# Second MLP: down products of two token blocks as seven products of 256 columns, in all four groups

## Chip, core and metric

The kernel runs on one NeuronCore of a Trainium2 chip. The metric is the device time of one execution in microseconds (us); of several runs the median is given. TensorE (PE) multiplies matrices, VectorE (DVE) and ScalarE (ACT) do elementwise work, SyncE (SP) issues the DMAs, GpSimd (POOL) works only in the first stage here.

## The reference, cut

```
out = decayed linear attention of q, k, v with lam
x   = out as [1536 tokens, 512]
x   = g1(x @ moe_w_in) @ moe_w_out     # [512, 2048], g1(h) = h * tanh(softplus(h)), [2048, 512]
y   = g2(x @ moe2_w_in) @ moe2_w_out   # the same shapes, g2(h) = max(h, 0) ** 2
```

All in 32-bit floats. The two MLPs are layers L = 0 and L = 1 of the kernel.

## The kernel before, in words

**Numbers in two parts.** Each operand of a product is held as a high part (a copy rounded to the matmul's type, made by ScalarE) and a low part (the difference, made by VectorE); `split` (L292) issues the two. `mm3` (L282) makes of each product three matmuls: high by low, low by high, high by high. All matmuls of the MLPs are issued at L289, all plain copies of ScalarE at L277 and all sums and differences of two tensors by VectorE at L280, so the tiles' names tell them apart in the trace.

**Tiles.** The 1536 tokens are three blocks t = 0, 1, 2 of 512. The inner width of 2048 is four groups g of 512. A *unit* is an SBUF tile of 128 x 1024 words of 4 bytes, and there are 51 (`UNITS`, L34). A PSUM tile is also 128 x 1024, over two banks, and there are four. For each layer and group: `weights` (L517) loads two units of each weight (kind 0 is w_in, kind 1 is w_out; the loads have 64-bit elements, which ScalarE, tile m, and VectorE, tile t, bring into 32 bits at L551, L556 and L563) and splits them into wh, wl. `up` (L677) makes the up products of block 0. `up_pair` (L725) makes those of blocks 1 and 2 together by seven products in place of eight, in the manner of Strassen: sums and differences of quarters of the weight (`sums`, L575, tiles s, sh, sl) meet sums and differences of quarters of the tokens (`forms`, L618, tiles T, fh, fl), and the products are put together in PSUM, on top of copies made by ScalarE (`seed`, L750) or by VectorE's sums. `gated` (L655) applies the activation.

**Down products.** `down` (L793) makes for one block two results (d = 0, 1), each of 24 matmuls for each of two units u. From the second group on, ScalarE first copies the sum so far from SBUF into PSUM (`onto`, L800), the matmuls add to it, and ScalarE copies it back (ac). For groups in `PAIRS` (L37: layer 0, groups 1 to 3) blocks 1 and 2 go instead through `down_pair` (L854): seven products again, each with a split of its own (eh, el), with the kind-1 sums of `sums` and the differences D of the gated units, and six sums kept from group to group (`keep`, tiles ap and ac). In layer 1 no group is in `PAIRS`: there blocks 1 and 2 go through `down`, 48 matmuls of 512 columns for each block and group, with tokens on the partitions of the result.

**Forms.** The 14 units fh, fl of a layer stay in SBUF in its first groups. From group `SPILL[L]` on (L39: 2 for layer 0, 9, which is never, for layer 1) `load_form` (L611) fetches each from DRAM just before its product, at most 14 us ahead (`BACK`); `store_form` (L605) has put them there (L608).

**Order.** No order is written by hand for most engines. Every operation is given to `Plan` (L64) with an engine, an estimated time, what it reads and writes, and for PE a rank; `ranks` (L962) counts them up. `dues` (L108) derives for every other operation the latest start that keeps PE going in rank order. `run` (L130) then plays the engines forward: PE takes the ready operation of lowest rank, another engine the one that is due first among those due within 40 us (`AHEAD`) for which a unit is free. A weight load of SP starts only if 10 units beside its own stay free, and the two operations that unpack it only if 6 do (`SPARE`, L41, L546, L559). The order so found is each engine's fixed queue.

**Sequence.** Per group: up of block 0, up_pair, then down of block 0 and either down_pair or down of blocks 1 and 2. Group (0, 0) goes block by block. `TURNED` (L29) is empty: a group in it would take up_pair ahead of up, and down_pair ahead of down. In the last group of layer 1 the last block handled is the tail (L795): its results come in halves of 512 columns, VectorE adds each to the sum so far, and SP stores it.

Of the kernel before, what the change touches and what calls it, by code (L numbers as in the profile page):

```python
# [25 lines left out]
TB = 512  # L26
WARM = 8
GF = 4
TURNED = ()  # L29

RANGE = 2.0 ** -112
BELOW = 2.0 ** 32
# [1 line left out]
UNITS = 51  # L34
STRASSEN = (True, True)
PLAIN = ((0, 0),)
PAIRS = ((0, 1), (0, 2), (0, 3))  # L37
DEBUG = None
SPILL = (2, 9)  # L39
BACK = 14.0  # L40
SPARE = (10, 6)  # L41
AHEAD = 40.0
# [21 lines left out]
class Plan:  # L64
# [7 lines left out]

    LAG = {"PE": 0.35, "DVE": 0.2, "ACT": 0.3, "POOL": 0.25, "SP": 3.8}

    def __init__(self, ahead):
        self.ops, self.ahead = [], ahead
        self.wrote, self.used, self.orders = {}, defaultdict(list), set()

    def op(self, eng, us, fn, reads=(), writes=(), name="", rank=None, lag=None, due=None, spare=0, ahead=None):
        o = Op(eng, us, fn, name, rank, self.LAG[eng] if lag is None else lag, due, spare)  # L80
        o.ahead = ahead or self.ahead.get(eng)
        for x in reads:
            o.before[self.wrote[x]] = None
        for x in writes:
            o.before.update(dict.fromkeys(self.used[x]))
            if x in self.wrote:
                o.before[self.wrote[x]] = None
        for x in reads:
            self.used[x].append(o)
        for x in writes:  # L90
            self.wrote[x], self.used[x] = o, []
        for x in (*reads, *writes):
            if isinstance(x[0], Val):
                o.vals[x[0]] = None
        for v in o.vals:
            v.left += 1
        for b in o.before:
            b.after[o] = None
        self.ops.append(o)
        return o  # L100
# [29 lines left out]
    def run(self, start, units):  # L130
# [5 lines left out]
        for o in self.ops:  # L136
            if not left[o]:
                o.at = 0.0
                ready[o.eng].append(o)
        releases, order, last = [], [], {}  # L140

        turn = {}
        for o in sorted((o for o in self.ops if o.eng == "PE"), key=lambda o: o.rank):
# [13 lines left out]
        while n < len(self.ops):  # L157
            while releases and releases[0][0] <= now:
                _, v = releases.pop(0)
                free[v.space].append(v.slot)  # L160
            for e in ready:
                if clock[e] > now:
                    continue
                can = [o for o in ready[e] if o.at <= now and (e == "PE" or o.late - now < o.ahead)]
                if not can:
                    continue
                best = None
                for o in sorted(can, key=lambda o: o.rank if e == "PE" else o.late):
                    need = defaultdict(int)
                    for v in o.vals:  # L170
                        if v.slot is None:
                            need[v.space] += 1
                    if any(v.seeded and v.slot is None and not fits(v) for v in o.vals):
                        continue
                    if o.eng != "PE" and need["P"] and next(v for v in turn if v.slot is None) not in o.vals:
                        continue
                    if all(len(free[s]) >= k + (o.spare if s == "S" else 0) for s, k in need.items()):
                        best = o
                        break
                if best is None:  # L180
                    continue
                o = best

                if e != "PE" and any(q.at > now and q.at < now + 0.7 * o.us and q.late < o.late - 2.0
                                     for q in ready[e]):
                    continue
                for v in sorted((v for v in o.vals if v.slot is None), key=lambda v: v.name):
                    v.slot = fits(v)[0]
                    free[v.space].remove(v.slot)
                    if v.space == "P":  # L190
                        last[v.slot] = v
                o.start, o.end = now, now + o.us
                clock[e] = o.end
                ready[e].remove(o)
                order.append(o)
                n += 1
                for v in o.vals:
                    v.left -= 1
                    v.was = max(v.was or 0.0, o.end + o.lag)
                    if not v.left:  # L200
                        bisect.insort(releases, (v.was, v), key=lambda r: r[0])
                for a in o.after:
                    left[a] -= 1
                    if not left[a]:
                        a.at = max(b.end + (b.lag if (b.eng != a.eng or b.lag > 1) and (b, a) not in self.orders else 0.0)
                                   for b in a.before)
                        ready[a.eng].append(a)
            times = [c for c in clock.values() if c > now]
            times += [o.at for r in ready.values() for o in r if o.at > now]
            times += [r[0] for r in releases[:1]]  # L210
            times += [o.late - o.ahead + 1e-6 for e in ready if e != "PE" for o in ready[e]
                      if o.late - o.ahead + 1e-6 > now]
            times = [t for t in times if t > now]
            if not times:
                stuck = [o.name for r in ready.values() for o in r][:20]
                held = sorted({v.name for o in self.ops for v in o.vals if v.slot is not None and v.left and v.space == "S"})
                raise RuntimeError(f"stuck {held} at {now} with {n} of {len(self.ops)}: {stuck} {len(free['S'])} {len(free['P'])}")
            now = min(times)
# [5 lines left out]
def attention_mlps(ctx, tc, lam, qk, kv, w_in, w_out, w2_in, w2_out, out):  # L224
# [292 lines left out]
    def weights(L, g, kind, kk):  # L517
# [4 lines left out]
        for i in range(2):  # L522
# [33 lines left out]
                    nc.vector.tensor_scalar(out=tl(t)[o, i], in0=tl(st, TB, 2)[r, :, 0], scalar1=29, scalar2=None,  # L556
                                            op0=ALU.logical_shift_right)

            op("ACT", 0.67 * len(rows()), high, [(st, 0)], [(m, i)], name=f"m{name}{i}", spare=SPARE[1])  # L559
            op("DVE", 0.45 * len(rows()), low, [(st, 0)], [(t, i)], name=f"t{name}{i}", spare=SPARE[1])  # L560

        def join():
# [92 lines left out]
    def gated(L, g, t, u, h, in_psum):  # L655

        name = f"{L}{g}{t}{u}"
        if not in_psum:
            op("ACT", 1.05, lambda: nc.scalar.activation(out=tl(h), in_=tl(h), func=AF.Relu if L else AF.Mish),
               [(h, 0)], [(h, 0)], name=f"r{name}")  # L660
        if L:
            op("ACT", 1.05, lambda: nc.scalar.activation(out=tl(h), in_=tl(h), func=AF.Square),
               [(h, 0)], [(h, 0)], name=f"sq{name}")
        if t and (L, g) in PAIRS:
            h_raw[L, g, t, u] = h
            return
        hi, lo = Val(f"gh{name}", dtype=F32R), Val(f"gl{name}", dtype=F32R)
        g_hi[L, g, t, u], g_lo[L, g, t, u] = hi, lo
        split(hi, lo, h, [(h, 0)])

    def take(L, g, t, u, src):
        h = Val(f"h{L}{g}{t}{u}")
        op("ACT", 1.05, lambda: nc.scalar.activation(out=tl(h), in_=tl(src), func=AF.Relu if L else AF.Mish),  # L673
           halves(src), [(h, 0)], name=h.name)
        gated(L, g, t, u, h, True)

    def up(L, g, t, rank):  # L677
# [114 lines left out]

    def down(L, g, t, rank):  # L793
        final = g == NG - 1
        tail = final and L == 1 and t == NB - 1  # L795
        for d in range(2):

            outs = [product_unit(f"dn{L}{g}{t}{d}{i}", not tail) for i in range(2 if tail else 1)]
            o = outs[0]
            onto = g > 0 and not tail  # L800
            if onto:
                a = accs[L, t, d]
                o.seeded = True
# [50 lines left out]
    def down_pair(L, g, rank):  # L854
# [1 line left out]
        b11, b21, b12, b22 = (h_raw[L, g, t, u] for t in (1, 2) for u in (0, 1))  # L856
        final = g == NG - 1
        opening = accs.get((L, "p"), None) is None
        if opening:
            c11, c21, c12, c22 = (accs[L, t, d] for t in (1, 2) for d in range(2))  # L860
            op("DVE", 1.25, lambda: tt(tl(c12), tl(c12), tl(c22), ALU.subtract), [*halves(c12), *halves(c22)],
               halves(c12), name=f"-c12{L}{g}")
# [8 lines left out]
        def product(i, raw, o):  # L871
# [7 lines left out]
            for s in range(2):  # L879
                def products(s=s):  # L880
                    for k in range(2):
                        f = slice(s * P, (s + 1) * P)
                        mm3(tl(o)[:, s], view(lh)[:, k, f], view(ll)[:, k, f], tl(rh)[:, k], tl(rl)[:, k],
                            k == 0, k == 1, onto=onto)

                reads = [(x, 0) for x in (lh, ll, rh, rl)] + ([(o, s)] if onto else [])
                op("PE", 1.37, products, reads, [(o, s)], name=f"Q{i}{L}{g}{s}", rank=rank + n[0])
                n[0] += 1
            return o

# [18 lines left out]
        def keep(i, o):  # L909
            a = acc[i] = acc[i] if i in acc else Val(f"ap{L}{i}")  # L910
            op("ACT", 1.05, lambda: copy(tl(a), tl(o)), halves(o), halves(a), name=f"k{i}{L}{g}")
            return a

        def result(t, d, o):
            a = x_raw[1, t, d] = Val(f"xr1{t}{d}")
            op("ACT", 1.05, lambda: copy(tl(a), tl(o)), halves(o), halves(a), name=a.name)

        sub(t3, b22, b12)
        sub(t1, b12, b11)
        sub(t2, b22, t1)  # L920
        sub(t4, b21, t2)
        a = product(1, b11, None)
        b = plus(a, acc[2], "b")
        if not final:
            keep(3, product(3, b22, seed(3)))
            product(2, b21, b)
# [20 lines left out]
        plus(a, acc[4])  # L947
        product(4, t4, a)
        result(1, 1, a)
        c = x_raw[1, 2, 1] = Val("xr121")  # L950
        op("DVE", 1.25, lambda: tt(tl(c), tl(e), tl(f), ALU.add), [*halves(e), *halves(f)], halves(c), name=c.name)
        plus(e, acc[3])
        product(3, b22, e)
        result(2, 0, e)
# [115 lines left out]
```

## Time and profile before

| | |
|---|---|
| median of 3 runs | 550.01 us (549.73 to 550.61) |
| the profiled execution's own time | 551.3 us |
| its span | 549.5 us |
| PE busy | 540.9 us (98%), 2950 matmuls |
| PE weight loads busy | 447.5 us (81%) |
| VectorE busy | 320.4 us (58%) |
| ScalarE busy | 373.3 us (68%) |
| DMA | 71.77 MB, mean 131 GB/s |

The span is the profiled part of an execution; its own time, 1.8 us longer, lies around it. In the tables by stage a figure in brackets behind a busy time is the number of instructions, PEclk is the granted clock of TensorE as a share of 2.4 GHz, and DMA is the mean busy share of the 16 DMA engines. A tile is named without its buffer's number, so dn<-wh,gl is a matmul that writes a down result from the moving tile wh and the stationary tile gl. The duration of a matmul contains its way through the array, and the matmuls overlap; the pace is the distance of two starts.

### The profile page before, as it was taken

The numbers are of one execution on the slowest core, as the hardware profiler recorded it, in microseconds if no ns is written. First come the engines' busy times: TensorE is split into PE (matmuls) and PEld (weight loads), VectorE is DVE, ScalarE is ACT, GpSimd is POOL, SyncE is SP. The second block draws the span as 40 slices with busy tenths as digits, with TensorE's granted clock in tenths as the row PEclk, the third lists the DMA queues.
The fourth block names the chain that finished last, engine by engine and source line by source line (L and its number), as shares of the span: only waits on it lengthen the run. The fifth ranks groups of instructions, "written<-read, shape, count | busy, mean of one in ns | idle before, by whom it ended". The sixth has DMA issues, their size and how long they took to land.

```text
span 549.5 us, 7237 instructions
## 1 busy us (share of the span) xinstructions
PE 540.9 (98%) x2950; PEld 447.5 (81%) x2950; DVE 320.4 (58%) x353; ACT 373.3 (68%) x413; POOL 31.8 (6%) x32
## 2 busy tenths in 40 slices
PE   7999999999999999999999999999999999999997
PEld 5898788888888888888878888888888888888885
DVE  6848686562686739787498886424361455333302
ACT  3637566593878789688995887458962898457920
POOL 2666100000000000000000000000000000000000
PEclk9999999999999999999999999999999999999999
DMA  8998003702799426971404021121134010300123
GB/s 313 408 409 251 3 0 114 269 1 76 285 335 410 140 57 199 348 246 48 154 0 154 1 78 38 51 103 39 38 116 151 3 38 1 115 2 1 38 78 115
DMA packets 20515, 71.77 MB, mean 131 GB/s; under 512 B 2306, under 2 KB 2306, under 8 KB 20482
## 3 DMA queue, kind: packets, MB, share of 16 engines
q1 hardware_dynamic: 20480, 71.31, 36.7%
q8 instruction: 23, 0.38, 0.3%
q14 instruction: 10, 0.08, 0.0%
q10 hardware_dynamic: 2, 0.00, 0.0%
HBM read 60.82 MB, written 10.49 MB: 130 GB/s over the span
## 4 chain that ended last, share of the span: by engine, by line
PE 91%; ACT 4%; DMA 2%; DVE 1%; issue 1%; SPq 0%; ACTq 0%
PE dn L289 34%; PE up L289 20%; PE p L289 13%; PE e L289 7%; PE b L289 4%; PE o L289 4%; PE q L289 3%; PE xo L455 2%; PE sc L413 2%; DMA qk<-in_qk_dram 2%; PE xo L464 1%; PE sd L436 1%; ACT L551 1%; ACT eh L277 1%; ACT h L673 1%
## 5 line engine op out<-in xcount | busy, mean ns | idle before, releaser
L280 DVE TENSOR_TENSOR gl<-h,gh 128x1024 fp32r<-128x1024 f32 x36 | 45.5, 1267 | 59.6 <-ACT gh L277 59.3
L277 ACT ACTIVATE ac<-dn 128x1024 f32<-128x1024 f32 x34 | 34.9, 1027 | 62.2 <-PE dn L289 60.9
L289 PE MATMUL dn<-wl,gh 128*128 128x512 f32 x192 | 74.7, 389 | 0.0
L289 PE MATMUL dn<-wh,gl 128*128 128x512 f32 x192 | 74.7, 389 | 0.0
L289 PE MATMUL dn<-wh,gh 128*128 128x512 f32 x192 | 74.7, 389 | 0.0
L563 DVE SCALAR_TENSOR_TENSOR t<-m,t 128x1024 int32<-128x1024 int32 x32 | 39.8, 1249 | 44.9 <-ACT m L551 44.7
L280 DVE TENSOR_TENSOR wl<-t,wh 128x1024 fp32r<-128x1024 f32 x32 | 38.8, 1222 | 21.3 <-ACT wh L277 21.2
L551 ACT ACTIVATE m<-st 128x512 f32<-128x512 f32 (+1 forms) x66 | 42.1, 665 | 6.7 <-DMA st<-in_moe_w_in_dram 6.5
L289 PEld LDWEIGHTS dn<-wl,gh 128*128 128x128 f32 x192 | 36.0, 188 | 7.5
L289 PEld LDWEIGHTS dn<-wh,gl 128*128 128x128 f32 x192 | 36.0, 188 | 7.5
L289 PEld LDWEIGHTS dn<-wh,gh 128*128 128x128 f32 x192 | 36.0, 188 | 7.4
L673 ACT ACTIVATE h<-up 128x1024 f32<-128x1024 f32 x20 | 20.5, 1027 | 26.6 <-PE up L289 26.6
L277 ACT ACTIVATE gh<-h 128x1024 fp32r<-128x1024 f32 x36 | 37.8, 1054 | 0.5
L289 PE MATMUL dn<-gl,wh 128*128 128x512 f32 x96 | 37.3, 389 | 0.0
L289 PE MATMUL dn<-gh,wl 128*128 128x512 f32 x96 | 37.3, 389 | 0.0
L289 PE MATMUL dn<-gh,wh 128*128 128x512 f32 x96 | 37.3, 389 | 0.0
L277 ACT ACTIVATE wh<-t 128x1024 fp32r<-128x1024 f32 x32 | 33.4, 1050 | 5.0 <-DVE t L563 4.9
L280 DVE TENSOR_TENSOR sl<-s,sh 128x1024 fp32r<-128x1024 f32 x20 | 24.2, 1222 | 8.1 <-ACT sh L277 8.0
L289 PE MATMUL up<-xh,wh 128*128 128x512 f32 (+1 forms) x80 | 28.0, 350 | 0.0
L289 PE MATMUL up<-xl,wh 128*128 128x512 f32 (+1 forms) x80 | 27.8, 348 | 0.0
L289 PE MATMUL up<-xh,wl 128*128 128x512 f32 (+1 forms) x80 | 27.7, 346 | 0.0
L556 DVE TENSOR_SCALAR t<-st 128x512 int32<-128x512 int32 (+1 forms) x66 | 26.6, 438 | 0.1
(167 smaller groups left out, 1244.6 us busy)
## 6 DMA issues: line engine op xcount, KB each, us to landing
st<-in_moe_w_out_dram SPq DMA_DIRECT2D x32, 512.0 KB, 4.1
st<-in_moe_w_in_dram SPq DMA_DIRECT2D x26, 512.0 KB, 5.3
fh<-f SPq DMA_DIRECT2D x14, 512.0 KB, 7.1
fl<-f SPq DMA_DIRECT2D x14, 512.0 KB, 7.1
qk<-in_qk_dram SPq DMA_DIRECT2D x12, 512.0 KB, 10.3
kv<-in_kv_dram SPq DMA_DIRECT2D x12, 512.0 KB, 10.4
f<-fh SPq DMA_DIRECT2D x7, 512.0 KB, 6.3
f<-fl SPq DMA_DIRECT2D x7, 512.0 KB, 6.2
```

The costliest lines, as they stand in the source:

```text
L277: nc.scalar.activation(out=o, in_=i, func=AF.Copy)
L280: nc.vector.tensor_tensor(out=o, in0=a, in1=b, op=alu)
L289: nc.tensor.matmul(out=out_, lhsT=a, rhs=b, start=start, stop=pieces or (last and i == 2), skip_group_check=not start if pieces else onto)
L413: nc.tensor.matmul(out=o[:, e, p], lhsT=t[r, 1, p], rhs=t[r, 0, p], start=True, stop=True)
L436: nc.tensor.matmul(out=o[e * D : (e + 1) * D, p], lhsT=t[:, p, 1 + e], rhs=t[:, p, 0 if e else 3], start=True, stop=True)
L455: nc.tensor.matmul(out=o[weighted(p, e), p, n], lhsT=v[:, p, 0 if e else 3], rhs=w[:, e, p], start=p % 2 == n == 0, stop=True, skip_group_ ...
L464: nc.tensor.matmul(out=o[weighted(h, e), h, n], lhsT=z[r, h], rhs=qd[r, h], start=False, stop=True, skip_group_check=True)
L551: nc.scalar.activation(out=tl(m)[o, i], in_=tl(st, TB, 2)[r, :, 1].bitcast(F32), func=AF.Prelu, scale=RANGE, alpha=BELOW)
L556: nc.vector.tensor_scalar(out=tl(t)[o, i], in0=tl(st, TB, 2)[r, :, 0], scalar1=29, scalar2=None, op0=ALU.logical_shift_right)
L563: nc.vector.scalar_tensor_tensor(out=tl(t), in0=tl(m).bitcast(I32), scalar=3, in1=tl(t), op0=ALU.logical_shift_left, op1=ALU.bitwise_or)
L673: op("ACT", 1.05, lambda: nc.scalar.activation(out=tl(h), in_=tl(src), func=AF.Relu if L else AF.Mish), halves(src), [(h, 0)], name=h.name)
```

## The change

Layer 1 joins `PAIRS` in all four groups: blocks 1 and 2 go through `down_pair`. There each of its seven products has, for layer 1, gated tokens as the stationary operand (blocks of 128) and 256 columns of weights as the moving one, 24 matmuls of 256 columns for a product where layer 0 has 12 of 512. Group (1, 0) has no earlier sums: its second accumulator starts as ScalarE's copy. The results of the last group go to the output straight from `down_pair` (four stores of 512 KB, rows of 1 KB). Block 0 of layer 1 is no longer accumulated in PSUM: VectorE adds each result to the sum (`ADDED`). Where a gated unit of layer 1 does not come from PSUM, one VectorE operation makes both relu and square. Layer 1's forms are stored and fetched again from its group 2 on (`SPILL`). Group (1, 3) is turned. The planner counts 1.5 us for a change of ScalarE's function table and ranks an operation that needs one 4 us later.

```diff
@@ -26,7 +26,8 @@
 GF = 4
-TURNED = ()
+TURNED = ((1, 3),)
+ADDED = (False, True)
@@ -34,9 +35,9 @@
 PLAIN = ((0, 0),)
-PAIRS = ((0, 1), (0, 2), (0, 3))
+PAIRS = ((0, 1), (0, 2), (0, 3), (1, 0), (1, 1), (1, 2), (1, 3))
 DEBUG = None
-SPILL = (2, 9)
+SPILL = (2, 2)
 BACK = 14.0
@@ -72,13 +73,15 @@
+    SWITCH = (1.5, 4.0)
+
     def __init__(self, ahead):
...
-    def op(self, eng, us, fn, reads=(), writes=(), name="", rank=None, lag=None, due=None, spare=0, ahead=None):
+    def op(self, eng, us, fn, reads=(), writes=(), name="", rank=None, lag=None, due=None, spare=0, ahead=None, table=None):
         o = Op(eng, us, fn, name, rank, self.LAG[eng] if lag is None else lag, due, spare)
-        o.ahead = ahead or self.ahead.get(eng)
+        o.ahead, o.table = ahead or self.ahead.get(eng), table
         for x in reads:
@@ -137,7 +140,7 @@
                 ready[o.eng].append(o)
-        releases, order, last = [], [], {}
+        releases, order, last, table = [], [], {}, None
@@ -165,7 +168,8 @@
                 best = None
-                for o in sorted(can, key=lambda o: o.rank if e == "PE" else o.late):
+                for o in sorted(can, key=lambda o: o.rank if e == "PE" else o.late + (
+                        self.SWITCH[1] if o.table and o.table != table else 0.0)):
                     need = defaultdict(int)
@@ -190,6 +194,8 @@
                 o.start, o.end = now, now + o.us
+                if o.table and o.table != table:
+                    o.end, table = o.end + self.SWITCH[0], o.table
                 clock[e] = o.end
@@ -556,7 +562,7 @@
-            op("ACT", 0.67 * len(rows()), high, [(st, 0)], [(m, i)], name=f"m{name}{i}", spare=SPARE[1])
+            op("ACT", 0.67 * len(rows()), high, [(st, 0)], [(m, i)], name=f"m{name}{i}", spare=SPARE[1], table="prelu")
             op("DVE", 0.45 * len(rows()), low, [(st, 0)], [(t, i)], name=f"t{name}{i}", spare=SPARE[1])
@@ -655,10 +661,13 @@
         name = f"{L}{g}{t}{u}"
-        if not in_psum:
+        if L and not in_psum:
+            op("DVE", 1.25, lambda: nc.vector.scalar_tensor_tensor(
+                out=tl(h), in0=tl(h), scalar=0.0, in1=tl(h), op0=ALU.max, op1=ALU.mult), [(h, 0)], [(h, 0)], name=f"rs{name}")
+        elif not in_psum:
             op("ACT", 1.05, lambda: nc.scalar.activation(out=tl(h), in_=tl(h), func=AF.Relu if L else AF.Mish),
-               [(h, 0)], [(h, 0)], name=f"r{name}")
-        if L:
+               [(h, 0)], [(h, 0)], name=f"r{name}", table=None if L else "mish")
+        if L and in_psum:
             op("ACT", 1.05, lambda: nc.scalar.activation(out=tl(h), in_=tl(h), func=AF.Square),
@@ -671,7 +680,7 @@
         op("ACT", 1.05, lambda: nc.scalar.activation(out=tl(h), in_=tl(src), func=AF.Relu if L else AF.Mish),
-           halves(src), [(h, 0)], name=h.name)
+           halves(src), [(h, 0)], name=h.name, table=None if L else "mish")
         gated(L, g, t, u, h, True)
@@ -792,12 +801,12 @@
         final = g == NG - 1
-        tail = final and L == 1 and t == NB - 1
+        tail = final and L == 1 and t == (0 if (L, g) in PAIRS else NB - 1)
         for d in range(2):
...
             o = outs[0]
-            onto = g > 0 and not tail
+            onto = g > 0 and not tail and not ADDED[L]
             if onto:
@@ -856,7 +865,9 @@
         opening = accs.get((L, "p"), None) is None
-        if opening:
+        if opening and not g:
+            accs[L, "p"] = {}
+        elif opening:
             c11, c21, c12, c22 = (accs[L, t, d] for t in (1, 2) for d in range(2))
@@ -879,12 +890,18 @@
                     for k in range(2):
+                        if L:
+                            for j in (2 * s, 2 * s + 1):
+                                f = slice(j * P, (j + 1) * P)
+                                mm3(tl(o, 4, 2 * P)[:, j], tl(rh)[:, k, f], tl(rl)[:, k, f], view(lh)[:, k], view(ll)[:, k],
+                                    k == 0 and j == 2 * s, k == 1, onto=onto, pieces=True)
+                            continue
                         f = slice(s * P, (s + 1) * P)
...
                 reads = [(x, 0) for x in (lh, ll, rh, rl)] + ([(o, s)] if onto else [])
-                op("PE", 1.37, products, reads, [(o, s)], name=f"Q{i}{L}{g}{s}", rank=rank + n[0])
+                op("PE", 1.42 if L else 1.37, products, reads, [(o, s)], name=f"Q{i}{L}{g}{s}", rank=rank + n[0])
                 n[0] += 1
@@ -911,16 +928,26 @@
+        def done(t, d, a):
+            if not L:
+                x_raw[1, t, d] = a
+                return
+            r = slice(t * TB, (t + 1) * TB)
+            op("SP", 1.3, lambda: nc.sync.dma_start(
+                out=out[r, d * 2 * P : (d + 1) * 2 * P].rearrange("(b p) c -> p b c", p=P), in_=tl(a, 4, 2 * P)),
+               halves(a), [("out", t, d)], name="out")
+
         def result(t, d, o):
-            a = x_raw[1, t, d] = Val(f"xr1{t}{d}")
+            a = Val(f"xr{L}{t}{d}")
             op("ACT", 1.05, lambda: copy(tl(a), tl(o)), halves(o), halves(a), name=a.name)
+            done(t, d, a)
...
         a = product(1, b11, None)
-        b = plus(a, acc[2], "b")
+        b = plus(a, acc[2], "b") if 2 in acc else copied(a, "b")
         if not final:
@@ -947,8 +974,9 @@
         result(1, 1, a)
-        c = x_raw[1, 2, 1] = Val("xr121")
+        c = Val(f"xr{L}21")
         op("DVE", 1.25, lambda: tt(tl(c), tl(e), tl(f), ALU.add), [*halves(e), *halves(f)], halves(c), name=c.name)
+        done(2, 1, c)
         plus(e, acc[3])
```

## Rows read from the trace of the kernel before

**Rows 1.** The page's busy times: engine, us, share of the span, instructions.

```profile
PE 540.9 (98%) x2950; PEld 447.5 (81%) x2950; DVE 320.4 (58%) x353; ACT 373.3 (68%) x413; POOL 31.8 (6%) x32
```

**Rows 2.** Busy times by stage of PE's order, us from the span's start.

```profile
core 0: us, PE busy (x) PEld busy (x) DVE busy (x) ACT busy (x) POOL busy (x), PEclk, DMA share, GB/s
13.67:71.76 58.09, 56.43 (x785) 48.62 (x786) 42.39 (x50) 34.88 (x52) 28.57 (x23) 1.00 0.69 254
...
175.12:234.96 59.84, 59.84 (x265) 49.55 (x265) 42.70 (x47) 49.67 (x53) 0.00 (x0) 1.00 0.60 204
234.96:281.95 46.99, 46.57 (x205) 38.19 (x205) 35.24 (x36) 42.25 (x44) 0.00 (x0) 1.00 0.36 118
281.95:325.47 43.52, 43.52 (x194) 36.04 (x193) 39.34 (x39) 32.67 (x35) 0.00 (x0) 1.00 0.15 49
325.47:358.11 32.64, 32.64 (x146) 27.03 (x145) 18.85 (x24) 20.85 (x24) 0.00 (x0) 1.00 0.24 75
358.11:420.67 62.56, 62.56 (x278) 51.80 (x277) 23.84 (x26) 41.18 (x44) 0.00 (x0) 1.00 0.20 68
```

**Rows 3.** The chain that ended last: start us, us, what.

```profile
27.75 8.83 PE up L289 x72
...
205.04 10.88 PE dn L289 x48
215.92 2.72 PE q L289 x12
...
325.47 32.64 PE dn L289 x144
...
545.83 0.69 DVE ac L280
```

**Rows 4.** Timeline in the attention stage, PE and its weight loads (PEld): start us, us.

```profile
28.02 0.28 PE L289 MATMUL up<-xl,wh 128*128 128x256 f32 x1
28.02 0.19 PEld L289 LDWEIGHTS up<-xh,wh 128*128 128x128 f32 x1
...
28.14 0.19 PEld L289 LDWEIGHTS up<-xh,wl 128*128 128x128 f32 x1
...
36.30 0.28 PE L289 MATMUL up<-xl,wh 128*128 128x256 f32 x1
```

**Rows 5.** Groups of DVE and ACT by form: count, busy us, mean ns, idle before.

```profile
L280 DVE TENSOR_TENSOR gl<-h,gh 128x1024 fp32r<-128x1024 f32 x36 | 45.5, 1267 | 59.6 <-ACT gh L277 59.3
L563 DVE SCALAR_TENSOR_TENSOR t<-m,t 128x1024 int32<-128x1024 int32 x32 | 39.8, 1249 | 44.9 <-ACT m L551 44.7
...
L551 ACT ACT_TABLE_LOAD x11 | 14.1, 1283 | 1.4 <-PEq L1057 1.3
...
L280 DVE TENSOR_TENSOR el<-h,eh 128x1024 fp32r<-128x1024 f32 x9 | 11.0, 1219 | 11.2 <-ACT eh L277 11.2
L277 ACT ACTIVATE eh<-h 128x1024 fp32r<-128x1024 f32 x9 | 9.5, 1056 | 0.1
...
L280 DVE TENSOR_TENSOR s<-t,t 128x512 f32<-128x512 f32 x10 | 6.9, 687 | 0.2
...
L280 DVE TENSOR_TENSOR b<-q,ac 128x1024 f32<-128x1024 f32 x3 | 3.7, 1228 | 0.7 <-PE q L289 0.7
```

**Rows 6.** SP's queue in time: start us, us, weight loads and a form's store.

```profile
144.86 1.21 SPq L608 DMA_DIRECT2D f<-fh  x1
...
292.41 5.50 SPq L544 DMA_DIRECT2D st<-in_moe_w_in_dram  x4
325.50 19.20 SPq L544 DMA_DIRECT2D st<-in_moe_w_out_dram  x4
```

**Rows 7.** DMA issues on the page: count, KB each, median us to landing.

```profile
st<-in_moe_w_out_dram SPq DMA_DIRECT2D x32, 512.0 KB, 4.1
...
fh<-f SPq DMA_DIRECT2D x14, 512.0 KB, 7.1
...
out_dram<-ac SPq DMA_DIRECT2D x4, 512.0 KB, 2.8
```

## Prediction

> **What bounds the kernel now.** I read the busy times first: PE is busy 540.9 of 549.5 us, and no other engine comes near [rows 1]. A busy share alone proves little, so I went on to the table by stage. In the stages from 175.12 to 420.67 us PE has no hole except 0.42 us in one of them (46.57 of 46.99 us), always at the full granted clock [rows 2]. The chain of waits says the same: in layer 1 it runs through nothing but PE, stage after stage, and ends with one VectorE add of 0.69 us [rows 3]. So the time is the number of matmuls times their pace, as long as the other engines keep up. Their headroom is large in layer 1: in group (1, 1), 62.56 us long, VectorE is busy 23.84 us and ScalarE 41.18 [rows 2]. The places to look at are the border between the layers (VectorE 39.34 of 43.52 us) and the first stage, where PE lacks 1.66 of 58.09 us [rows 2].
>
> **What the change does to PE.** Each group of layer 1 now has 144 down matmuls of 512 columns in 32.64 us [rows 3] (three more such steps follow), which is 0.2267 us each. 48 of them stay with block 0. The other 96, for 96 x 0.2267 = 21.76 us, become 7 products of 24 matmuls of 256 columns, 168 in all. The price of one is the main term. The trace has this very shape, in the first up products: 128 x 256 moving, each with its own 128 x 128 stationary tile, the same three-part products. From the start at 28.02 to the start at 36.30 us lie 69 steps, 8.28 us, so 0.1200 us each [rows 4]. That is 256 columns at 2.4 GHz, 0.1067 us, and 0.0133 more; 512 columns have the same 0.0133 on top of 0.2133. So 168 x 0.1200 = 20.16 us: **1.60 us less in each group, 6.40 us in four.** The bounds: half the 512-column pace (no charge for a matmul of its own), 0.1133 us, gives 19.04 and 10.9 us in four groups; the whole early step, 72 matmuls in 8.83 us with its start-up [rows 3], 0.1226 us, gives 20.60 and 4.6 us. I take 0.1200, the steady pace of the same form.
>
> Of the seven products only one in eight is saved, and two fifths of that are lost again on the shorter matmuls: seven products of 512 columns would take 7 x 2.72 = 19.04 us, as in layer 0 [rows 3].
>
> The Trainium skill (TensorE: Matmul & The Clock Gate, "Wait — 56ns, not 53.3ns?") gives a warm start-to-start of N / 2.4 GHz and about 2.5 ns. By it the estimate would be 96 x 0.2158 - 168 x 0.1092 = 2.4 us a group, 9.5 in all. This trace has 13.3 ns in place of 2.5, at both widths, and the measurement decides.
>
> **ScalarE and VectorE in layer 1.** Per middle group ScalarE loses 12 copies (two for each of six results), 4 high parts gh and the relu and square of one unit; it gains 2 sh, 7 eh, 4 seeds and 6 kept sums: 18 go and 19 come, at about 1.05 us [rows 5]. VectorE loses 4 gl (1.27 us each) and gains 4 weight sums (0.69), 2 sl, 7 el and 4 differences (1.22 each), the sums onto q and b (2 of 1.23), 2 adds for block 0 (1.23) and one relu-and-square: +2.7 +15.9 +4.9 +1.25 -5.1 = 19.7 us [rows 5]. That last form is not in the trace; the nearest two-tensor operations are 1.22 and 1.27 us, and it stands on no path that either end would change. Group (1, 1) would so have ScalarE at about 42 and VectorE at 43.5 of 60.96 us. Layer 0's stage of the same work had 49.67 and 42.70 of 59.84 us and PE without a hole [rows 2]. So I cost all of it at nothing; the cover is PE's 10.88 us of block 0's down, which stands between up_pair and down_pair.
>
> **The border, group (1, 0).** VectorE works 39.34 + 18.85 = 58.2 us there [rows 2], in 74.6 us after the change. It gains 4 sums, 2 sl, 7 el, 4 differences, one relu-and-square and loses 4 gl: 2.7 + 15.9 + 1.25 - 5.1 = 14.8 us (group 0 adds nothing onto earlier sums). That makes 73 of 74.6 us, but part of it prepares group (1, 1)'s kind-1 weights, not needed before 30 us later. I cost it at nothing, with up to 3 us for the range.
>
> **Smaller parts.** 14 stores of forms take 1.2 us each of SP's queue [rows 6], some 17 us, ahead of weight loads that are not needed for 40 us or more; 28 loads come back in 7.1 us [rows 7], under a DMA share that was 0.60 in layer 0's group with the same loads. Nothing. The turn of group (1, 3) brings its kind-0 sums and first forms forward by block 0's 10.88 us; VectorE has the room. The results of the last down_pair leave before the 10.88 us of block 0's down; a store of 512 KB took 2.8 us, and with the form's slower 7.1 us [rows 7] it is still over in time. The tail is the same: halves, one add of 0.69 us, one store. The planner's count of table loads may reorder ScalarE in layer 0 (11 loads of 1.28 us at L551 alone [rows 5]); PE can win there the 0.42 us hole and part of the 1.66 us, and lose as much: I take 0.
>
> **Sum.** 549.5 - 6.4 = 543.1 us of span, 551.3 - 6.4 = 544.9 us for an execution like the profiled one. The median of the runs is 1.3 us under that execution, so 550.0 - 6.4 = **543.6 us**.
>
> **The rivals.**
>
> *Part of it is given back at the border.* VectorE's 73 of 74.6 us in (1, 0) make PE wait for a split or for the next weights. For: VectorE is busier there than in any other stage shown, before the change already [rows 2]. Against: the later weights can slip. One to four microseconds lost: 544.6 to 547.6 us, up to 548.9 with holes at both borders.
>
> *Units run out: slower.* In layer 0 the 14 units of forms were gone by the time of a down_pair; in (1, 0) they stay for (1, 1). Beside them are 4 units of block 0's input, 8 of kind-1 weights and sums, 8 of gated units and differences, 4 of splits, and by the end 8 of sums: 46 of 51, where a weight load wants 11 free. If the four w_in loads of (1, 1), issued at 292.41 us before [rows 6], would have to wait for the end of down_pair, PE would stand for a landing (4.1 us [rows 7]), a joining and a low part for each of two units (1.25 and 1.22) and a high part (1.06 [rows 5]): about 8.9 us, net 2.5 slower: 552.5 us. It decides from 7.5 us of standing on. Against: before, they were issued 65 us ahead of their use, while units were free, and nothing before that point is changed.
>
> *Weight loads bind.* A load shows 0.19 us [rows 4], and 256 columns last only 0.107. If a load could not run beside the matmul ahead of it, 168 would take at least 31.6 us, 9.8 more than now, 39 us in all: 589 us. The trace speaks against it: loads start every 0.12 us [rows 4]. The Trainium skill (the same page, "The mechanism", under what overlaps) has loads beside running matmuls only in other row groups; all are full here, and the rows contradict it.
>
> *The pace is half that of 512 columns*, 0.1133 us: 10.9 us less, 539.1 us. Against it stand the rows of the very shape [rows 4].
>
> *It doesn't do what it says in time*: the turned last group or the forms' loads cost what the products save; then 549 to 551 us.
>
> **How the numbers follow.** Over 0.2% (1.1 us) a measurement of this kernel can tell from no change. Forecast as summed, 542.4 (0.42 and half of 1.66 won) to 545.3 (the slower pace): 0.66. Part given back: 0.16. No change: 0.05. Units: 0.08. Weight loads: 0.02. Half pace: 0.03. Faster is 0.66 + 0.16 + 0.03 = 0.85, same 0.05, slower 0.10. The range from 542.4 to 547.5 takes in the forecast and most of the second case, about 0.8.
>
> **What would show it.** Right: starts of the layer-1 q, o, b, e matmuls 0.120 us apart, a down_pair of 20.16 us in four places, PE without holes from (1, 0) on, four groups of 60.96 us. Wrong: a PE hole behind VectorE's el or D at 325 to 360 us (the border), a hole at the first up matmul of (1, 1) with its w_in loads issued after 340 us (units), a hole at the first products of (1, 3) behind a form's load (the turn), or another pace.

## The result, and the profile after

The changed kernel takes 543.68 us (median of 4 runs, 542.96 to 543.87) against 550.31 us before: a ratio of 0.9875, 95% interval 0.9857 to 0.9893. The forecast was 543.6 us.

The page gives the busy time of each engine. Here is that line of the changed kernel:

```profile
PE 532.1 (98%) x3238; PEld 454.4 (84%) x3238; DVE 394.8 (73%) x426; ACT 376.7 (70%) x418; POOL 31.4 (6%) x32
```

PE has 288 matmuls more than before and is busy 8.8 us less [rows 1]; 2.2 of these lie ahead of the first mark below, in a part that scatters from one execution to the next. VectorE has 74.4 us more to do, ScalarE 3.4. The table by stage, cut where PE's order changes from up to down or from group to group:

```profile
core 0: us, PE busy (x) PEld busy (x) DVE busy (x) ACT busy (x) POOL busy (x), PEclk, DMA share, GB/s
...
233.10:279.34 46.24, 46.24 (x205) 38.29 (x205) 35.46 (x36) 39.96 (x42) 0.00 (x0) 1.00 0.34 114
279.34:322.86 43.52, 43.52 (x193) 36.04 (x193) 39.09 (x40) 33.35 (x35) 0.00 (x0) 1.00 0.15 49
322.86:353.89 31.03, 31.03 (x217) 29.16 (x217) 26.77 (x30) 23.92 (x27) 0.00 (x0) 1.00 0.22 68
353.89:414.87 60.98, 60.98 (x349) 53.94 (x349) 46.02 (x49) 44.24 (x48) 0.00 (x0) 1.00 0.79 298
...
475.85:536.91 61.06, 61.05 (x348) 53.59 (x347) 42.81 (x43) 34.69 (x36) 0.00 (x0) 1.00 0.14 48
```

Two readings answer [rows 2]. Group (1, 1) takes 60.98 us in place of 62.56, PE without a hole, although VectorE is busy 46.02 us there in place of 23.84. And the stage ahead of the border, 46.99 us with a hole of 0.42, is 46.24 us with none.

The chain of waits shows the products themselves, in group (1, 1) and at the end:

```profile
383.84 10.88 PE dn L295 x48
394.72 2.87 PE q L295 x24
...
409.11 5.76 PE o L295 x48
414.87 10.91 PE up L295 x48
...
527.20 2.87 PE e L295 x24
530.07 6.84 PE dn L295 x30
...
536.93 0.69 DVE ac L286
```

From 394.72 to 414.87 us: 20.15 us for seven products. In the last group PE takes matmuls of block 0's down (dn) between the last products (e). The timeline of PE, at the first product of (1, 0), gives the pace: 20 steps from 333.57 to 335.97 us, 0.120 us each, as the early up products had [rows 4].

```profile
333.57 0.28 PE L295 MATMUL q<-wl,eh 128*128 128x256 f32 x1
333.69 0.28 PE L295 MATMUL q<-wh,el 128*128 128x256 f32 x1
...
335.97 0.28 PE L295 MATMUL q<-wh,eh 128*128 128x256 f32 x1
```

**Where the time went.** Three marks in PE's order cut an execution so that single tenths can be compared: the start of the first down products, (0, 0); the start of the down products of (1, 0); and the start of the last add. Before, the chain has them at 71.76, 325.47 and 545.83 us; after, at 69.90, 322.86 and 536.93.

- Between the second and the third mark lies layer 1 from its first down products on: 220.36 us before, 214.07 after, **6.29 us less**. Four times 1.60 was 6.40.
- Between the first and the second: 253.71 and 252.96, **0.75 us less**.
- Ahead of the first mark the profiled executions scatter: 69.73 and 69.90 in two of the changed kernel, 69.92 to 71.34 in the variants below, most of which leave that stage alone. What is gained or lost there in one execution is not the change's.

6.29 + 0.75 = 7.04 us; the medians differ by 6.63 with an uncertainty of about 1 us.

### The profile page after: what moved, and what is told of

It is laid out like the page before. It is cut to its first block, busy times and chain, and to the rows that moved or that the text cites. A ratio compares the mean times of both kernels' runs of the same rounds, so it can differ in the third digit from the quotient of the medians.

```text
span 540.8 us, 8018 instructions
## 1 busy us (share of the span) xinstructions
PE 532.1 (98%) x3238; PEld 454.4 (84%) x3238; DVE 394.8 (73%) x426; ACT 376.7 (70%) x418; POOL 31.4 (6%) x32
## 4 chain that ended last, share of the span: by engine, by line
PE 97%; DMA 2%; SPq 0%; DVE 0%; issue 0%
PE up L295 20%; PE dn L295 20%; PE p L295 14%; PE q L295 11%; PE e L295 9%; PE o L295 9%; PE b L295 7%; PE xo L461 2%; PE sc L419 2%; DMA qk<-in_qk_dram 2%; PE xo L470 1%; PE sd L442 1%; DVE a L286 0%; SPq L408 0%; SPq L550 0%; SPq L406 0%
## 5 line engine op out<-in xcount | busy, mean ns | idle before, releaser
L286 DVE TENSOR_TENSOR sl<-s,sh 128x1024 fp32r<-128x1024 f32 x28 | 34.1, 1222 | 12.9 <-ACT sh L283 12.9
L286 DVE TENSOR_TENSOR gl<-h,gh 128x1024 fp32r<-128x1024 f32 x20 | 25.0, 1259 | 18.9 <-ACT gh L283 18.1
L286 DVE TENSOR_TENSOR el<-D,eh 128x1024 fp32r<-128x1024 f32 x28 | 33.7, 1220 | 2.3 <-ACT eh L283 2.1
L283 ACT ACTIVATE eh<-D 128x1024 fp32r<-128x1024 f32 x28 | 29.0, 1051 | 6.2 <-DVE D L286 6.0
L286 DVE TENSOR_TENSOR el<-h,eh 128x1024 fp32r<-128x1024 f32 x21 | 25.3, 1220 | 10.2 <-ACT eh L283 10.2
L283 ACT ACTIVATE sh<-s 128x1024 fp32r<-128x1024 f32 x28 | 29.2, 1051 | 2.0 <-DVE s L286 2.0
L283 ACT ACTIVATE ac<-dn 128x1024 f32<-128x1024 f32 x14 | 14.4, 1027 | 22.1 <-PE dn L295 22.1
L295 PE MATMUL dn<-wl,gh 128*128 128x512 f32 x64 | 24.9, 390 | 0.0
L295 PE MATMUL dn<-wh,gl 128*128 128x512 f32 x64 | 24.9, 390 | 0.0
L295 PE MATMUL up<-yl,wh 128*128 128x512 f32 x64 | 24.9, 389 | 0.0
```

What stands on the lines that cost most here:

```text
L283: nc.scalar.activation(out=o, in_=i, func=AF.Copy)
L286: nc.vector.tensor_tensor(out=o, in0=a, in1=b, op=alu)
L295: nc.tensor.matmul(out=out_, lhsT=a, rhs=b, start=start, stop=pieces or (last and i == 2), skip_group_check=not start if pieces else onto)
```

## The experiments

All runs but three change one thing in the changed kernel. The bold figure is the median; layer 1 means the distance of the second and the third mark, 214.07 us for the changed kernel.

**The planner alone.** The kernel before with `SWITCH` and the two table names, nothing else.

> The kernel before with the planner's count of table changes alone. Theory (the products carry the gain; the planner is worth next to nothing): 549.6 to 550.3 us, that is 0 to 0.7 us less; the 0.42 us hole of PE ahead of the layers' border goes. Rival (the planner carries what the profiled span lost beyond the products' 6.4 us, that is 2.3 us): 547.5 to 548.5 us.

**549.6 us**, ratio 0.9983 (0.9974 to 0.9992). Layer 1 takes 220.36 us, as before; from the first to the second mark 252.96, as after. So the count of table loads is worth 0.75 us and the seven products do the rest. PE's timeline of the kernel before shows what these 0.75 us were:

```profile
278.09 0.39 PE L289 MATMUL q<-eh,wh 128*128 128x512 f32 x1
278.89 0.50 PE L289 MATMUL o<-el,sh 128*128 128x512 f32 x1 [0.42 <-ACT o L277]
279.24 0.40 PE L289 MATMUL o<-eh,sl 128*128 128x512 f32 x1
```

The hole is shown as 0.42 us because a matmul's shown duration reaches beyond the start of the next. The two starts around it lie 0.80 us apart where the pace is 0.227, so 0.57 us are lost there; the first step behind it takes 0.35 us, 0.12 more; the next eleven steps together lose the other 0.06.

**The other way round:** the changed kernel without the count.

```diff
-    SWITCH = (1.5, 4.0)
+    SWITCH = (0.0, 0.0)
```

> The changed kernel without the planner's count of table changes. Theory: 543.7 to 544.4 us, the 0.42 us hole ahead of the border is back. Rival (the count carries 2.3 us): 545.5 to 546.5 us.

**544.62 us**, ratio 0.9903 (0.9887 to 0.9918). 253.69 us between the first two marks, so 0.73 us are back; layer 1 at 214.08 has not moved. The median lies 0.2 us above the theory's range. The rival of 2.3 us falls in both runs.

**Wide products.** Does PE's pace set the time, or have the other engines no more to give?

```diff
-                        if L:
-                            for j in (2 * s, 2 * s + 1):
...
-                            continue
-                op("PE", 1.42 if L else 1.37, products, ...)
+                op("PE", 1.37, products, ...)
```

> The changed kernel with layer 1's seven products as 12 matmuls of 512 columns, as in layer 0; the sums of blocks 1 and 2 then lie transposed and the stored values of these blocks are not the reference's. Theory (the time is PE's matmuls times their pace): a product takes 12 x 0.2267 = 2.72 in place of 24 x 0.1200 = 2.88 us, 28 products, 4.5 us less than the change: 539.2 us. Rival (VectorE and ScalarE, busier now, hold PE back as soon as it is faster): 541 to 543.7 us, with holes of PE in layer 1.

**538.48 us**, ratio 0.9791 (0.9778 to 0.9805). Layer 1 takes 209.47 us, 4.60 less than the change where 4.48 was worked out, still without a hole of PE; the median lies 0.7 us below the one expected. The step from one pace to the other is a matter of PE alone.

**Three groups in place of four.**

```diff
-PAIRS = (..., (1, 0), (1, 1), (1, 2), (1, 3))
+PAIRS = (..., (1, 1), (1, 2), (1, 3))
```

> The changed kernel with group (1, 0) taken out of the pairs, so three groups of seven products; the first group's sums of blocks 1 and 2 are arranged otherwise than the later ones, so these blocks' values are not the reference's. Theory (1.60 us a group): 543.7 + 1.6 = 545.3 us. Rival (the border's group costs in VectorE's work what it saves): 543.7 us or less.

**545.0 us**, ratio 0.9909 (0.9896 to 0.9923). Layer 1 takes 215.65 us: 1.58 us more, one group's 1.60. The border group pays as any other.

**VectorE's cover taken away.** The prediction set VectorE's 20 us more per group at nothing. Here each of the seven low parts of a group is made twice.

```diff
             split(rh, rl, raw, [(raw, 0)])
+            if L:
+                op("DVE", 1.25, lambda: tt(tl(rl), tl(raw), tl(rh).bitcast(F32), ALU.subtract),
+                   [(raw, 0), (rh, 0)], [(rl, 0)], name=f"again{rl.name}")
```

> The changed kernel with every subtraction el of layer 1's down_pair made twice, 7 more VectorE operations of 1.22 us in each group, 8.5 us; VectorE would be busy some 54.6 of 60.98 us in groups (1, 1) and (1, 2) and 35 of 31.03 us in the down part of (1, 0). Theory (VectorE's work is covered, with 15 us to spare a group): 543.7 us, at most 545. Rival (the cover is thin at the border, where the next group's wl was ready 2.4 us ahead of its use): 546 to 550 us, with the holes of PE at the first up matmuls of (1, 1).

**557.95 us**, ratio 1.0145 (1.0129 to 1.016): 14.3 us lost, more than either side expected. Both were wrong: the cover is not 15 us a group, and the loss is not at the border alone. The chain of that run in group (1, 1), once PE has to wait:

```profile
402.32 2.89 PE b L295 x24
405.24 1.03 ACT ap L283
406.27 0.95 ACT eh L283
407.24 1.24 DVE el L286
...
408.50 1.23 DVE el L286
...
409.78 3.01 PE q L295 x23
```

A product waits for its own split: ScalarE's kept sum, then the high part, then two low parts. This can be read in two ways, as a longer chain or as too much work for VectorE, and two runs look into it.

**The same work beside the path.** The extra operations write a tile that nothing reads, and the planner gives them a due time 1 us behind that of their product.

```diff
+                beside.append(op("DVE", 1.25, lambda: tt(tl(spare), tl(rl).bitcast(F32), tl(rh).bitcast(F32), ALU.subtract),
+                                 [(rl, 0), (rh, 0)], [(spare, 0)], name=f"beside{rl.name}"))
...
+            if hasattr(o, "behind"):
+                o.late = o.behind.late + 1.0
```

> The changed kernel with as many extra VectorE operations as in the run that made el twice, 7 of 1.22 us in each group of layer 1, but beside the path: nothing waits for their result, the planner gives them a late due time, and they hold one unit more. If VectorE's time itself had run out there, about the same loss: 554 to 558 us. If the loss came from the longer chain of a split ahead of its product: 543.7 to 547 us.

**559.31 us**, ratio 1.0165 (1.015 to 1.018). Nothing waits for the results of these operations, and the loss is as large, even 1.3 us above the range that was expected for it. So more work for VectorE is enough for the loss, without a longer split. The table of this run from the first up matmuls of (1, 1) to those of (1, 2), and on to the first b matmuls of (1, 3), with the columns of the table above:

```profile
358.68:421.76 63.08, 61.55 (x350) 53.98 (x349) 53.24 (x56) 44.60 (x48) 0.00 (x0) 1.00 0.82 304
421.76:497.17 75.41, 70.35 (x380) 61.53 (x379) 64.48 (x70) 49.41 (x53) 0.00 (x0) 0.95 0.42 147
```

The busy share of VectorE is only 84 and 86% there (53.24 of 63.08 and 64.48 of 75.41 us), and yet PE stands: the work is not spread evenly. The chain at the end of (1, 1) names it:

```profile
412.36 1.09 DVE t L564 x3
413.45 1.13 DVE spare L288
414.58 1.14 DVE el L288
...
416.77 1.22 DVE t L571
417.99 1.13 DVE spare L288
419.13 1.15 DVE wl L288
...
420.32 1.45 PE p L297 x5
```

In one queue stand the last splits of this group and the unpacking (t) and the low part (wl) of the next group's weights. The extra tile also takes one of the 51 units. That isn't what (1, 1) waits for: the last w_in loads of (1, 2) go out at 383.90 us, as those of the changed kernel do at 383.87, and the run with el twice, which has no such tile, needs nearly the same for the group (62.81 and 63.08 us). The extra operations also read el and eh and so hold their units longer; what this and the extra unit cost in the later groups was not measured.

Part of the loss is TensorE's clock. PE stands 4.65 us in (1, 2), and the 23 matmuls behind that take 5.01 us where 23 behind a shorter wait took 3.01 (above):

```profile
483.27 5.01 PE o L297 x23
```

From 483.30 to 487.40 us the granted clock is 0.50, the lower of its two levels (1.2 GHz), and from 487.90 us on 1.00 again. That is 2.0 us, and it is what the 0.95 in the table stands for. With el twice there is such a stretch in the last group: 23 matmuls from 536.21 us on take 4.46 us, at a granted clock of 0.56 from 536.20 to 540.00.

**One group alone.** El twice only in (1, 1).

> The changed kernel with el made twice in group (1, 1) alone. If each group pays for itself, as its stage of 62.81 in place of 60.98 us in the earlier run reads: 545 to 546 us. If only the pile of delays over the groups cost: 543.5 to 544.5 us.

**545.35 us**, ratio 0.991 (0.9893 to 0.9926). Layer 1 takes 216.44 us, 2.37 us more than the change, for 8.5 us of VectorE's work. So a group pays for itself. In its chain PE waits for a split that now has two low parts (the product at 408.85 us) and for the next group's wl (418.06), so here the longer split and VectorE's time are not told apart. Four such groups would lose 9.5 us; all four together lost 14.67 in layer 1. The starts of PE's b matmuls divide an execution by group (us):

| from, to | changed | el twice | beside the path | el twice in (1, 1) |
|---|---|---|---|---|
| down of (1, 0), b of (1, 1) | 50.10 | 51.93 | 52.26 | 50.10 |
| b of (1, 1), b of (1, 2) | 60.98 | 62.81 | 63.08 | 63.34 |
| b of (1, 2), b of (1, 3) | 50.10 | 55.25 | 57.70 | 50.10 |
| b of (1, 3), last add | 52.89 | 58.75 | 56.30 | 52.90 |

In the two runs with more work in every group the first two stages lose about 2 us each and the later ones 3.4 to 7.6, in which one stretch at the lower clock makes 1.5 us (el twice) and 2.0 us (beside the path).

**Parts of the change undone.** First the turn of the last group.

```diff
-TURNED = ((1, 3),)
+TURNED = ()
```

> The changed kernel with group (1, 3) in the order of the others, so that down_pair is last. Theory (at the end nothing is left to cover down_pair's chain of sums, copies and splits): PE stands between the last products, 546 to 549 us. Rival (the turn is neutral, as the prediction costed it): 543.2 to 544.2 us.

**546.1 us**, ratio 0.9934 (0.992 to 0.9947). 2.4 us are lost. The chain of that run, in the last down_pair, which is now the end:

```profile
525.48 2.89 PE q L295 x24
...
528.45 1.02 ACT e L283
...
529.51 3.14 PE e L295 x24
...
538.45 1.02 ACT xr L283
```

In the turned order PE fills these waits with block 0's down matmuls (the dn between the e of the chain after). The wait is only about half of it: from the first down products of (1, 0) to its last matmul's end PE takes 215.39 us in place of 214.05. The rest lies behind the last matmul, 5.1 us to the end of the span in place of 3.9: there stand a copy of a whole result (1.02 us) and a store of 512 KB, where the turned order has an add of half a result (0.69) and a store of 256 KB. The prediction called the turn neutral; it is worth about a third of the gain.

**Block 0 seeded again.**

```diff
-ADDED = (False, True)
+ADDED = (False, False)
```

> The changed kernel with block 0 of layer 1 accumulated in PSUM again: in each of three groups 4 ScalarE copies in place of 2 VectorE adds. Theory (both engines are covered): 543.4 to 544.2 us. Rival (ScalarE, 44 of 61 us, becomes late with 4 us more): 545 us or more.

**543.78 us**, ratio 0.9883 (0.9868 to 0.9898); layer 1 214.08 us, the change's to 0.01. Whether VectorE or ScalarE does it costs nothing.

**Forms kept in SBUF.**

```diff
-SPILL = (2, 2)
+SPILL = (2, 9)
```

> The changed kernel with layer 1's 14 units of forms kept in SBUF to the end: no stores, no loads. Theory (units are what binds the order: with 14 fewer free, the weights of groups (1, 2) and (1, 3) are unpacked late): 546 to 556 us, with holes of PE at the first up matmuls of a group. Rival (the DMAs of forms cost as much as they free): 543.2 to 544.2 us.

**551.7 us**, ratio 1.003 (1.002 to 1.0039): without the stores and loads of forms the seven products are a loss. The chain has two holes of PE, each ahead of a group's first matmuls; this is the first:

```profile
410.07 2.89 PE o L295 x24
...
412.99 1.03 ACT ap L283
414.01 1.14 ACT m L557 x2
...
415.18 1.23 DVE t L569
416.41 1.15 DVE wl L286
...
417.60 2.83 PE p L295 x11
```

Here (1, 2)'s weights are unpacked (m, t) only when the products of (1, 1) have ended. The loads say why. SP's queue of that run, and then of the changed kernel:

```profile
401.46 2.14 SPq L550 DMA_DIRECT2D st<-in_moe_w_in_dram  x3
```

```profile
288.38 4.91 SPq L550 DMA_DIRECT2D st<-in_moe_w_in_dram  x4
...
353.68 0.33 SPq L550 DMA_DIRECT2D st<-in_moe_w_in_dram  x1
...
383.87 1.51 SPq L550 DMA_DIRECT2D st<-in_moe_w_in_dram  x3
```

With 14 units fewer free, the same three loads go out 16.6 us later, counted from the first down products of (1, 0) (323.82 us in that run). The second hole is 4.75 us, at the first products of (1, 3), and the matmuls behind it are slow:

```profile
483.68 9.85 PE p L295 x35
```

Their granted clock is 0.51 from 483.70 to 487.00 us. At the full clock they would have taken about 8.2 us, an estimate from 23 such matmuls behind a wait (5.51 us at 491.65 in the run beside the path) and 12 more (2.72). Layer 1 takes 222.60 us in this run, 8.5 more than in the changed kernel: 1.6 of these are the clock, the others the two holes. Units are what the stores buy.

**A version that beats both.** Wide products, and the four finished results of blocks 1 and 2 turned back by TensorE: eight transposes of 128 x 128 each, one more copy by ScalarE.

```diff
+            def turns():
+                for j in range(4):
+                    for s in range(2):
+                        nc.tensor.transpose(tl(o, 4, 2 * P)[:, j, s * P : (s + 1) * P],
+                                            tl(a)[:, s, j * P : (j + 1) * P], tl(same, 8, CH)[:, 0])
```

> The products of 512 columns, with the four results of blocks 1 and 2 turned back by 32 transposes of 128 x 128 on TensorE at the end, so that the output is the reference's. The wide products gave 5.2 us against the change. If a transpose goes at the pace of 0.12 us or less, 3.8 us are spent again at most and it beats the change: 540.5 to 543.3 us. If it takes 0.25 us or more, or the results' way through PSUM holds up the end: 544 us or more.

**542.29 us** (541.89 to 543.23), ratio 0.9858 (0.9843 to 0.9873). The chain shows the transposes:

```profile
514.70 0.87 PE tr L937 x8
515.57 1.38 PE dn L295 x6
...
529.64 0.87 PE tr L937 x8
530.51 6.83 PE dn L295 x30
```

0.87 us for eight, 0.109 us each, 3.48 in all, against 4.48 won. Layer 1 takes 213.07 us: 1.00 less than the change, as the sum says.

**The change once more,** beside that.

> The changed kernel itself once more, to set the kernel with the transposes against it. If the wide products with their transposes are really faster by their own count (4.5 us won, 3.5 spent): 543.2 to 543.9 us here against 542.3 there. If the two are the same: 542 to 542.8 us here.

**543.92 us** (542.38 to 545.0), ratio 0.9897 (0.988 to 0.9913); layer 1 214.07 us again. The interval of the turned-back version's ratio lies below this one and overlaps that of the changed kernel's first runs; the 1.00 us rests on the marks in the traces, which agree to 0.01 us between the two executions of the changed kernel.

## Why the prediction was right, point by point

- **The main term** held: 0.120 us a matmul, 20.15 us for seven products, 1.58 us for a group taken out, 6.29 us in four groups. The missing 0.11 us sits in the seams, where the first matmuls of 512 columns behind those of 256 take 0.03 us more (10.91 in place of 10.88 us) and in the mixed order of the last group. Both bounds are out. So is the shorter pace that the Trainium skill gives (TensorE: Matmul & The Clock Gate, "Wait — 56ns, not 53.3ns?"), by which it would have been 9.5 us, an estimate. (The section on down products ahead of the prediction gives 24 matmuls for each result and unit; it is 12, which makes the 48 for a block that the chain shows and the prediction uses.)
- **The closeness of the number** is partly chance. 543.6 was forecast and 543.68 measured, but the marks show 7.04 us where 6.4 were summed, and the median of before was 550.31 beside the change, 0.3 above the one that the sum started from.
- **The planner** was costed at 0, with 0.42 us as the most to win at that hole. It won 0.75: 0.57 us between the two starts around the hole, and 0.18 in the steps behind it.
- **VectorE's and ScalarE's sums** in (1, 1) came to 46.02 and 44.24 us, 43.5 and 42 were worked out. "I cost all of it at nothing" held for the time. The reason given, a stage of layer 0 that was as busy without a hole of PE, was enough for this load and says nothing of what is left: a quarter of VectorE's time is free in (1, 1), 15 us, but 8.5 us more of its work in that group cost 2.37 us.
- **The border.** 73 of 74.6 us were worked out as the worst for VectorE; it was busy 39.09 + 26.77 = 65.9, because part of (1, 1)'s kind-1 weights slipped behind the border, as the prediction allowed. The cover was thin all the same. The second wl of (1, 1) ends at 341.6 us before, 16.5 ahead of its use at 358.11; after, at 351.45, 2.4 us ahead of 353.89. The rows are of VectorE's timeline, before and after:

```profile
339.13 2.44 DVE L280 TENSOR_TENSOR wl<-t,wh 128x1024 fp32r<-128x1024 f32 x2
```

```profile
350.23 1.22 DVE L286 TENSOR_TENSOR wl<-t,wh 128x1024 fp32r<-128x1024 f32 x1 [1.11 <-ACT wh L283]
```

- **Units** were the right kind of rival, put in the wrong place. At (1, 0) the w_in loads of (1, 1) went out at 288.38 us, as early as before, and only their unpacking came late. The place where units decide is (1, 2) and (1, 3), and there the change itself pays for them with `SPILL`. "Nothing" for the stores and loads was right as a cost and missed what they are for: 8.0 us (551.7 against 543.7). The price of this rival was also added up wrongly: with a joining and a low part for each of two units, as it says, 4.1, 2.5, 2.4 and 1.1 make 10.1 us and not 8.9, so 553.7 us. As the loads went out early, no run shows this price.
- **The turn** was costed as neutral, and the tail as the same. Both hold for the order that the change has; without the turn the end would have cost 2.4 us, half of it behind PE's last matmul.
- **Weight loads** did not bind: 0.120 us between matmuls that each have a load of their own.

## What to carry to other kernels

Where one engine has no holes, a saving on it can be read from a single pace in its own trace, and the whole question is whether the others still deliver. Judge that by the margin of each delivery (when wl ended, when PE wanted it), not by a busy share: an engine that is 75% busy may have little to give where it counts. Of a change with several parts, ask of each what the others would be worth without it; here two parts that save no matmul, the spill and the turn, cost 8.0 and 2.4 us when each was taken out by itself.

## What the runs showed of the hardware

- A short wait of PE costs more than the hole that is shown. At the hole of 0.42 us two starts lie 0.80 us apart, 0.57 more than the pace, and the first step behind it took 0.35 us in place of 0.227. Behind the waits of other runs the first step between matmuls of 256 columns was 0.22 or 0.23 us in place of 0.120 (at 409.78 us with el twice, at 529.51 without the turn). The granted clock of the first of these stages reads 1.00 [rows 2]; why the first step is longer was not tried.
- Behind three waits the granted clock of TensorE was at its lower level for a stretch: 0.50 from 483.30 to 487.40 us in the run beside the path, where PE had stood 4.65 us; 0.51 from 483.70 to 487.00 with the forms kept, where it had stood 4.75 us; 0.56 from 536.20 to 540.00 with el twice, where it had stood 1.71 and 0.74 us with one matmul between. In the first of them matmuls of 256 columns started 0.214 us apart in place of 0.120.
- A transpose of 128 x 128 of 32-bit words on TensorE took 0.109 us in a stream of eight, less than a matmul of 256 columns, and PE went on beside it without a hole.
